# A gated state-space and feed-forward mix on one core: readouts of 12 row blocks moved to ScalarE and adding transfers, two chunks of x turned by VectorE and SyncE transfers

## The chip, the core and the metric

The kernel runs on one core of a Trainium2 chip. A core has TensorE (matmuls, results in PSUM), VectorE (DVE), ScalarE (ACT), GpSimd (POOL) and SyncE (SP). Each takes its instructions in the order in which they stand in its own stream, and waits on semaphores for the others. Transfers are issued by SyncE, ScalarE or GpSimd and are carried out by 16 DMA engines that all of them share. The metric is the device time in microseconds, the median of several runs.

## The reference

x is 2048 tokens of 448 features. Two results are computed from it and mixed row by row with a gate.

```
g = sigmoid(sum(x * gate_w))                       # one number a token
dt = exp(log_dt);  Lam_bar = exp(dt * Lambda)      # 448 complex states
Bu = x @ (((Lam_bar - 1) / Lambda)[:, None] * B).T
h[t] = Lam_bar * h[t-1] + Bu[t]                    # over 2048 tokens
a = 2 * Re(h @ C.T) + x * Dskip
b = silu(x @ w1) @ w2                              # 448 -> 1792 -> 448
out = g * a + (1 - g) * b
```

## The kernel before

**Chunks.** The tokens go in 4 chunks of 512 (`tc`), each of 4 row blocks of 128 (`tb`, 16 in all). x lies in `xnat` with tokens on the partitions. The products need it with features on the partitions: `xT`, 4 groups of 128 features (the fourth overlaps the third by 64).

**Turning x.** Chunk 0 is turned by `x0_transposes`, chunks 1 to 3 by `x_transposes(tc, who)`: 32 small transposes on TensorE into two PSUM banks (line 508), then two copies out of PSUM, by VectorE (516) or ScalarE (518). They stand in the list of products at a place given by hand (`fill`).

**Products.** `x_products` takes a list of tiles two at a time. A tile is 128 columns of w1 (`F(tc)`, 14 tiles a chunk) or 64 states of B as real and imaginary part (`B(tc)`, 7 tiles). A pair of tiles takes 14 matmuls on 64 rows (663) into two banks; the first half of pair k+1 is put ahead of the second half of pair k. `evict` brings F tiles through silu into `aT` on ScalarE, and B tiles into `UG`, on VectorE for chunk 0 and on ScalarE for the others.

**The recurrence.** `lanes(tc)` multiplies by cosines and sines (704), so that a real decay is left, scans along the tokens with it (736, seven scans a chunk), casts the result with GpSimd's transfers from `Gf` into `UG` (390), and turns back with the same sines into `H[tc]`. For chunk 0 the products before the scans are made slot by slot (lines 712 to 725), for the others on whole tiles. `gin` carries the state to the next chunk.

**Parameters.** `parameters` makes decay, sines and cosines from three rows that are loaded into `prm`, turned by four tiny matmuls on TensorE (536).

**The sums.** `gates(tc)` makes the gate and puts g * x * Dskip into `Tb`, which is the same memory as `xnat`. `ffn2(tb)` is the second product of the feed-forward part (774): ScalarE scales it by 1 - g into `fe` (780), and GpSimd's transfer adds `fe` to `Tb` (782). `readout(tb)` is the product of the states with C (795): VectorE makes g * product + `Tb` into `ot` (798), and SyncE stores `ot` (801). The last row block is cut in three.

**Order.** The body at lines 864 to 883 lists the work as TensorE does it. `P.add` notes every instruction with what it reads and writes, a cost and a priority. `Plan.order` plays this through: TensorE keeps the listed order; on the other engines the one that can start first goes next, and among those the lowest priority number. The streams are fixed before the kernel runs. Names (`xT2_0`, `H3_5`) stand for pieces of memory: a reader waits for the last writer, a writer for all readers.

`H[3]` also serves as the landing place of B (`Bnat`) at the start. `ct` holds two pairs of f32 rows for the readout weights (`readout_weights`, 822 and 825, used by 827 and 830).

Of the kernel before, what the change touches and what calls it, by code (L numbers as in the profile page):

```python
# [7 lines left out]
ALU = mybir.AluOpType  # L8
# [268 lines left out]
def bass_gated_mix__ssm_conv_s5__dense_activation_silu__prompt_kernel(nc, A_x, A_Lambda_re, A_Lambda_im, A_B_re, A_B_im, A_C_re, A_C_im,  # L277
               A_log_dt, A_Dskip, B_x, B_w1, B_w2, gate_w, out):
    with ExitStack() as ctx:
# [114 lines left out]
        def load_w1(q, k, a, b):  # L394

            cols = slice(w1cuts[k], w1cuts[k + 1])
            src = B_w1[320:448, cols] if a == 3 else B_w1[128 * a:128 * b, cols].rearrange("(b p) f -> p b f", p=128)
            load(q, w1s[:, 3, cols] if a == 3 else w1s[:, a:b, cols], src, " ".join(f"w1_{k}_{i}" for i in range(a, b)),
                 256 * (b - a) * (cols.stop - cols.start))
# [12 lines left out]
        load("sp", Bnat[:, 0:3, :], A_B_re[0:384, :].rearrange("(b p) d -> p b d", p=128), "H3_0 H3_1 H3_2", 384 * 896)  # L412
# [55 lines left out]
        def x0_transposes(q0, part, who):  # L468

            tk = Ps(2)  # L470

            def mm(pe):
                for q in (q0, q0 + 1):
                    for k in range(2):
                        o = ((q - q0) * 2 + k) * 64
                        for h in range(2):
                            p = slice(64 * h, 64 * h + 64)
                            r = pe.transpose(bk(tk, h).bitcast(BF16)[:, o:o + 64], xnat[p, 2 * part + k, XCOL[q]:XCOL[q] + 128], ident[p, p])  # L478
                return r
# [14 lines left out]

        xn_of = {tc: {q: [f"xT{tc}_{h}" for h in range(2)] for q in range(4)} for tc in range(1, NCH)}
        xn_of[0] = {q: [f"xT0_{q}{part}{h}" for part in range(2) for h in range(2)] for q in range(4)}

        def x_transposes(tc, who):
# [13 lines left out]
            for h in range(2):  # L512
                src = lambda h=h: bk(tk, h).bitcast(BF16).rearrange("p (q b n) -> p q b n", q=4, b=4)
                dst = xT[:, :, tc * CH:(tc + 1) * CH].rearrange("p q (b h n) -> p q b h n", h=2, n=64)[:, :, :, h, :]
                if who[h] == "d":
                    DVE(lambda e, src=src, dst=dst: e.tensor_copy(dst, src()), [tk], [f"xT{tc}_{h}"], 0.69, 2.2, "xTe")
                else:
                    ACT(lambda e, src=src, dst=dst: e.activation(dst, src(), AF.Copy), [tk], [f"xT{tc}_{h}"], act_cost(1024), 2.2, "xTe")

        cosn = [f"COS{k}" for k in range(4)] + ["COSd"]  # L520
# [126 lines left out]
        def x_products(tiles, fill={}, wait=()):  # L647
# [10 lines left out]
            def steps(k, h, a, z):  # L658
                def body(pe):
                    for n, cut in list(enumerate(part[h]))[a:z]:  # L660
                        for b, ((i, p0), tile) in enumerate(zip(cut, pairs[k])):
                            tc = tile[1]
                            r = pe.matmul(bk(toks[k], b), weights(tile, p0, p0 + 64, i), xT[p0:p0 + 64, i, tc * CH:(tc + 1) * CH],  # L663
                                          start=(h == 0 and n == 0), stop=(h == 1 and n == 2))
# [41 lines left out]
        def lanes(tc):  # L706
# [4 lines left out]
            t = f"L{tc}"  # L711
            if tc == 0:
                for b in range(4):
# [12 lines left out]
            else:  # L726
# [59 lines left out]
        def readout(tb):  # L786
# [3 lines left out]
            for n, (a, b) in enumerate(cuts):  # L790
                tk = Ps()

                def mm(pe, tk=tk, a=a, b=b):
                    for s in range(NSLOT):
                        r = pe.matmul(bk(tk)[:, 0:b - a], H[tc][:, s, o:o + 128], CP[:, s, a:b], start=(s == 0), stop=(s == NSLOT - 1))  # L795
                    return r
                PE(mm, [f"H{tc}_{s}" for s in range(7)] + [f"CP{s}" for s in range(NSLOT)], [tk], NSLOT * (0.0025 + (b - a) / 2400), f"C{tc}")
                DVE(lambda e, tk=tk, a=a, b=b: e.scalar_tensor_tensor(ot[tb % NOT][:, a:b], bk(tk)[:, 0:b - a], g[:, tb:tb + 1],  # L798
                                                                      Tb[:, tb, a:b], ALU.mult, ALU.add),
# [61 lines left out]
        def C(*tbs):  # L861
# [17 lines left out]
        x_products(F(2, 1) + B(3) + F(3), {1: xt(3, "aa"), 9: [lambda: gates(3), lambda: lanes(3)]})  # L879
        for f in C(4, 5, 6, 7) + G(8, 9, 10, 11):  # L880
# [38 lines left out]
```

## Time and profile before

| what | us |
|---|---|
| median of 3 runs (141.49 to 141.81) | 141.78 |
| the profiled execution, its own time | 141.25 |
| its span, first to last instruction | 139.5 |
| TensorE, both products with xT (663) | 48.5 + 25.8 |
| TensorE, second feed-forward product (774) | 43.2 |
| VectorE, all scans (736), 28 of them | 33.8 |
| ScalarE, silu out of PSUM (634) | 28.7 |

The granted TensorE clock was 0.998 of full speed. The span is the stretch that the profile tells of; the rest of the time lies around it. Of the products with xT two matmuls on 64 rows run side by side, so a pair of them follows the last pair after 0.216 us though each is shown as 0.376. How full the DMA engines were, and what the queues did:

```profile
DMA  4998999510156770104976200674202322323242
q0 software_dynamic: 6064, 5.51, 24.8%
q1 hardware_dynamic: 11318, 8.65, 20.7%
```

The first line has the mean busy share of the 16 DMA engines in 40 equal slices of the span, in tenths. q0 is GpSimd's queue, q1 SyncE's: packets, megabytes, and their time as a share of all 16 engines' span. The loads fill the engines in the first fifth of the span; later there are mostly GpSimd's casts and adds.

### The profile page before, as it was taken

The numbers are of one execution on the slowest core, as the hardware profiler recorded it, in microseconds if no ns is written. First come the engines' busy times: TensorE is split into PE (matmuls) and PEld (weight loads), VectorE is DVE, ScalarE is ACT, GpSimd is POOL, SyncE is SP. The second block draws the span as 40 slices with busy tenths as digits, with TensorE's granted clock in tenths as the row PEclk, the third lists the DMA queues.
The fourth block names the chain that finished last, engine by engine and source line by source line (L and its number), as shares of the span: only waits on it lengthen the run. The fifth ranks groups of instructions, "written<-read, shape, count | busy, mean of one in ns | idle before, by whom it ended". The sixth has DMA issues, their size and how long they took to land.

```text
span 139.5 us, 3000 instructions
## 1 busy us (share of the span) xinstructions
PE 135.9 (97%) x1201; PEld 67.0 (48%) x1201; DVE 122.0 (87%) x179; ACT 90.3 (65%) x157; POOL 39.2 (28%) x72
## 2 busy tenths in 40 slices
PE   7999999999999999999999999999999999999992
PEld 2445454455544544455544544444455555555561
DVE  0319999999999999999999999999999999997053
ACT  3349768999989999823694887799931268312300
POOL 7134040100248440227733001824000314022220
PEclk9999999999999999999999999999999999999999
DMA  4998999510156770104976200674202322323242
GB/s 136 337 294 243 363 320 238 177 42 0 31 79 94 129 110 1 38 15 73 157 131 155 38 5 0 95 133 79 38 4 97 66 33 36 83 83 61 40 94 71
DMA packets 17956, 14.71 MB, mean 105 GB/s; under 512 B 2835, under 2 KB 17814, under 8 KB 17942
## 3 DMA queue, kind: packets, MB, share of 16 engines
q0 software_dynamic: 6064, 5.51, 24.8%
q1 hardware_dynamic: 11318, 8.65, 20.7%
q10 hardware_dynamic: 560, 0.36, 0.8%
q8 instruction: 9, 0.15, 0.4%
q14 instruction: 5, 0.04, 0.1%
HBM read 7.17 MB, written 1.84 MB: 65 GB/s over the span
## 4 chain that ended last, share of the span: by engine, by line
PE 97%; DVE 0%; issue 0%
PE ps L663 46%; PE ps L774 31%; PE ps L795 15%; PE ps L463 2%; PE ps L508 1%; PE ps L478 1%; PE ps L814 1%; PE ps L604 1%; DVE ot L798 0%; PE ps L675 0%; PE ps L464 0%; PE ps L536 0%
## 5 line engine op out<-in xcount | busy, mean ns | idle before, releaser
L663 PE MATMUL ps<-xT,w1s 64*128 64x512 bf16 x392 | 48.5, 378 | 0.0
L774 PE MATMUL ps<-w2s,aT 128*128 128x448 bf16 x224 | 43.2, 353 | 0.0
L634 ACT ACTIVATE aT<-ps 128x1024 bf16<-128x1024 f32 (+1 forms) x30 | 28.7, 969 | 8.5 <-PE ps L663 8.4
L774 PEld LDWEIGHTS ps<-w2s,aT 128*128 128x128 bf16 x224 | 21.7, 98 | 20.4 <-ACT xnat L849 0.4
L663 PEld LDWEIGHTS ps<-xT,w1s 64*128 64x128 bf16 x392 | 19.7, 94 | 22.3 <-DVE xT L486 0.7
L663 PE MATMUL ps<-xT,BT 64*128 64x512 bf16 x196 | 25.8, 376 | 0.0
L782 POOL DMA_DIRECT2D xnat<-fe x16 | 14.1, 900 | 37.9 <-ACT fe L780 37.2
L780 ACT ACTIVATE fe<-ps,g 128x448 bf16<-128x448 f32 x16 | 10.1, 632 | 21.1 <-PE ps L774 21.0
L390 POOL DMA_DIRECT2D UG<-Gf x27 | 14.7, 549 | 20.9 <-DVE Gf L736 20.4
L736 DVE TENSOR_TENSOR_SCAN Gf<-rc,gin,H 128x512 f32<-128x512 f32 x14 | 17.2, 1268 | 0.0
L795 PE MATMUL ps<-CP,H 128*128 128x448 bf16 (+2 forms) x98 | 16.4, 326 | 0.0
L663 PEld LDWEIGHTS ps<-xT,BT 64*128 64x128 bf16 x196 | 10.8, 94 | 11.1 <-DVE Gf L562 0.2
L798 DVE SCALAR_TENSOR_TENSOR ot<-ps,g,xnat 128x448 bf16<-128x448 f32 (+2 forms) x18 | 10.8, 622 | 6.0 <-issue 4.6
L390 POOL DMA_DIRECT2D UG<-UG x8 | 4.8, 597 | 29.2 <-ACT UG L642 17.4
L704 DVE TENSOR_TENSOR H<-UG,COS 128x3584 bf16<-128x3584 bf16 (+4 forms) x10 | 12.6, 1266 | 0.0
L795 PEld LDWEIGHTS ps<-CP,H 128*128 128x128 bf16 x98 | 8.9, 98 | 7.5 <-DVE k L752 0.4
L642 ACT ACTIVATE UG<-ps 128x1024 bf16<-128x1024 f32 (+1 forms) x12 | 10.7, 923 | 1.4 <-PE ps L663 1.4
L842 ACT ACTIVATE junk<-xg 128x448 bf16<-128x448 bf16 x16 | 9.2, 574 | 2.1 <-DVE xg L704 2.0
L849 ACT ACTIVATE xnat<-xnat,g 128x448 bf16<-128x448 bf16 x16 | 9.8, 671 | 0.2
L704 DVE TENSOR_TENSOR PI<-UG,SIN 128x512 bf16<-128x512 bf16 (+2 forms) x13 | 9.1, 722 | 0.0
L704 DVE TENSOR_TENSOR PO<-UG,SIN 128x1536 bf16<-128x1536 bf16 (+1 forms) x8 | 8.7, 1087 | 0.1
L736 DVE TENSOR_TENSOR_SCAN Gf<-rc,gin,H2C 128x512 f32<-128x512 f32 x7 | 8.5, 1265 | 0.0
(102 smaller groups left out, 126.5 us busy)
## 6 DMA issues: line engine op xcount, KB each, us to landing
UG<-Gf POOLq DMA_DIRECT2D x21, 128.0 KB, 2.5
xnat<-fe POOLq DMA_DIRECT2D x16, 112.0 KB, 2.6
out_dram<-ot SPq DMA_DIRECT2D x15, 112.0 KB, 1.7
w2s<-in_B_w_dram SPq DMA_DIRECT2D x1, 1568.0 KB, 11.8
xnat<-in_A_x_dram SPq DMA_DIRECT2D x3, 448.0 KB, 6.1
w1s<-in_B_w_dram SPq DMA_DIRECT2D x1, 576.0 KB, 6.2
UG<-UG POOLq DMA_DIRECT2D x8, 64.0 KB, 2.2
H2C<-in_A_C_re_dram SPq DMA_DIRECT2D x2, 196.0 KB
```

Of the source, the lines that this page charges most:

```text
L390: P.add(q, lambda e: e.dma_start(dst, src), list(after), name.split(), 0.6 if q == "pool" else 0.5, prio, sem(), nbytes, tag="ld " + name)
L634: ACT(lambda e, src=src, dst=dst: e.activation(dst, src(), AF.Silu), [tk, "tbl"], [f"aT{tc % 2}_{m}" for m in names], act_cost(512 * n), 2 ...
L642: ACT(lambda e, src=src, dst=dst: e.activation(dst, src(), AF.Copy), [tk], [f"{un}{m}" for m in names], act_cost(512 * n), 5, "U")
L663: r = pe.matmul(bk(toks[k], b), weights(tile, p0, p0 + 64, i), xT[p0:p0 + 64, i, tc * CH:(tc + 1) * CH], start=(h == 0 and n == 0), stop=( ...
L704: DVE(lambda e: e.tensor_tensor(o, a, b, op), r, w, dve_cost(n, 2), prio, tag)
L736: DVE(lambda e, s=s, b=b, init=init: e.tensor_tensor_scan(Gf[:, s, :], rc[:, b:b + 1].to_broadcast([128, CH]), A[:, s, :], init, ALU.mult, ...
L774: r = pe.matmul(bk(tk)[:, 0:D_MOD], aT[tc % 2][:, fb, o:o + 128], w2s[:, fb, :], start=(fb == 0), stop=(fb == NFB - 1))
L780: ACT(lambda e: e.activation(f[:, :], bk(tk)[:, 0:D_MOD], AF.Copy, scale=g1[:, tb:tb + 1]), [tk, f"g1_{tc}"], [fn], act_cost(448, 1), 7, "fe")
L782: P.add("pool", lambda e: e.dma_start(Tb[:, tb, :], f[:, :], accum_op=ALU.add), [fn, f"Tb{tb}"], [f"Tb{tb}"], 0.94, 2, sem(), 115000, tag= ...
L795: r = pe.matmul(bk(tk)[:, 0:b - a], H[tc][:, s, o:o + 128], CP[:, s, a:b], start=(s == 0), stop=(s == NSLOT - 1))
L798: DVE(lambda e, tk=tk, a=a, b=b: e.scalar_tensor_tensor(ot[tb % NOT][:, a:b], bk(tk)[:, 0:b - a], g[:, tb:tb + 1], Tb[:, tb, a:b], ALU.mul ...
L849: ACT(lambda e, tb=tb: e.activation(Tb[:, tb, :], xnat[:, tb, :], AF.Copy, scale=g[:, tb:tb + 1]), [f"xd{tc}", f"g_{tc}"], [f"Tb{tb}"], ac ...
```

## The change

- Chunks 2 and 3 are no longer turned by TensorE. `x_blocks(tc)` turns 32x32 blocks on VectorE into a scratch in `H[3]` (4 instructions), and 16 transfers on SyncE's queue bring each block of rows to its place in `xT`, 32 partitions and 64-byte runs at a time. The turning of chunk 2 is ordered behind a product of chunk 0's lanes (`PI_0`), that of chunk 3 behind chunk 0's result (`H0_0`); both use the same scratch.
- The readouts of row blocks 0 to 11 are scaled by g out of PSUM by ScalarE into `ct` (f32). GpSimd's transfer adds them to `Tb`, and SyncE stores `Tb` itself. Blocks 12 to 15 stay as they were.
- Chunk 0's lanes are made on whole tiles as the others are.
- w1's loads are cut otherwise (two halves a column group, the second of which takes feature groups 2 and 3 in one transfer; the second column group partly on ScalarE's queue), the parameter rows are loaded ahead of w1's third column group, and `parameters` stands half a pair earlier in TensorE's list. Chunk 1 is turned one pair earlier, and chunk 0's lanes are listed one pair later.
- `xT` is laid out chunk by chunk.

```diff
+L0M = True
+XT1K = 6
+S0 = (0, 4, 1, 5, 2, 6, 3)
+XT1 = "da"
+XPRIO = {2: 15, 3: 20.5}
+XBLK = (2, 3)
+XBEH = {2: "PI_0", 3: "H0_0"}
+UDVE = (0, 1, 2, 3, 4, 5, 6)
+OUTA = tuple(range(12))
+PRMF = (0, 0)
...
-        xT = sb("xT", [128, 4, S_TOK], BF16)
+        xT = sb("xT", [128, NCH, 4, CH], BF16)
...
-        load_w1("sp", 0, 0, 2)
-        load_w1("act", 0, 2, 3)
-        load_w1("act", 0, 3, 4)
-        for k in range(1, len(w1cuts) - 2):
-            load_w1("sp", k, 0, 3)
-            load_w1("sp", k, 3, 4)
+        for k in range(2):
+            load_w1("sp", k, 0, 2)
+            load_w1("act", k, 2, 4)
         for k, v in enumerate((A_log_dt, A_Lambda_re, A_Lambda_im)):
             load("sp", prm[k:k + 1, 0:448], v.rearrange("(o n) -> o n", o=1), f"prm{k}", 896)
+        load_w1("sp", 2, 0, 2)
+        load_w1("sp", 2, 2, 4)
...
+        def x_blocks(tc):
+            X32 = H[3][:, 0:4, :].rearrange("p m (q b i) -> p m q b i", q=4, i=32)
+            names = [f"X32_{k}" for k in range(4)]
+            held = [f"H3_{s}" for s in range(7)] + ["H3_3i"]
+            turned = [f"BT{s}_{h}" for s in range(7) for h in range(2)]
+            xs = xnat[:, 4 * tc:4 * tc + 4, :]
+            for k, (q0, q1, c, b0, b1) in enumerate(((0, 3, 0, 0, 2), (0, 3, 0, 2, 4), (3, 4, XCOL[3], 0, 2), (3, 4, XCOL[3], 2, 4))):
+                n = q1 - q0
+                src = xs[:, b0:b1, c:c + 128 * n].rearrange("p b (q m i) -> p b q m i", q=n, i=32)
+                dst = X32.rearrange("p m q b i -> p b q m i")[:, b0:b1, q0:q1, :, :]
+                DVE(lambda e, dst=dst, src=src: e.transpose(dst, src), [f"xn{tc}", XBEH[tc]] + turned, [names[k]], 0.15 + 256 * n / 960, XPRIO[tc], "xTd")
+            k = sem()
+            for g in range(4):
+                for m in range(4):
+                    to = xT[32 * m:32 * m + 32, tc, :, :].rearrange("p q (b g i) -> p (q b) g i", b=4, i=32)[:, :, g, :]
+                    P.add("sp", lambda e, to=to, g=g, m=m: e.dma_start(to, X32[32 * g:32 * g + 32, m, :, :, :].rearrange("p q b i -> p (q b) i")),
+                          names + held, [f"xT{tc}_{g}{m}"], 0.66, 400, k, 32768, tag="xTm")
...
-            if tc == 0:
+            if tc == 0 and not L0M:
...
+                if tb in OUTA:
+                    f, fn = ct[tb // 2 % 2][:, tb % 2, :], f"ct{tb // 2 % 2}{'ab'[tb % 2]}"
+                    ACT(lambda e, tk=tk, f=f: e.activation(f, bk(tk)[:, 0:D_MOD], AF.Copy, scale=g[:, tb:tb + 1]),
+                        [tk, f"g_{tc}"], [fn], act_cost(448, 1), 3, "out")
+                    P.add("pool", lambda e, f=f: e.dma_start(Tb[:, tb, :], f, accum_op=ALU.add), [fn, f"Tb{tb}"], [f"Tb{tb}"], 0.94, 2, sem(), 230000, tag="Tb+")
+                    P.add("sp", lambda e: e.dma_start(out2[t0:t0 + 128, :], Tb[:, tb, :]), [f"Tb{tb}"], [], 0.3, 1, outs[tb % NOT], 128 * 896, tag="st")
+                    continue
...
-                   {(1, 0): [parameters], (K - 2, 0): turn_b[:1], K - 2: turn_b[1:2], K - 1: turn_b[2:], 7: xt(1, "da") + [lambda: lanes(0)]}, [K - 2])
+                   {PRMF: [parameters], (K - 2, 0): turn_b[:1], K - 2: turn_b[1:2], K - 1: turn_b[2:], XT1K: xt(1, XT1), 8: [lambda: lanes(0)] + [lambda: x_blocks(2)] * (2 in XBLK)}, [K - 2])
...
+        if 3 in XBLK:
+            x_blocks(3)
-        x_products(F(1) + F(2, 0, 1) + B(2), {2: xt(2, "aa")})
+        x_products(F(1) + F(2, 0, 1) + B(2), {2: xt(2, "aa")} if 2 not in XBLK else {})
...
-        x_products(F(2, 1) + B(3) + F(3), {1: xt(3, "aa"), 9: [lambda: gates(3), lambda: lanes(3)]})
+        x_products(F(2, 1) + B(3) + F(3), {1: xt(3, "aa") if 3 not in XBLK else [], 9: [lambda: gates(3), lambda: lanes(3)]})
```

More of the change, by code (lines that the diff above doesn't have):

```diff
@@ L396, in load_w1 @@
             cols = slice(w1cuts[k], w1cuts[k + 1])
-            src = B_w1[320:448, cols] if a == 3 else B_w1[128 * a:128 * b, cols].rearrange("(b p) f -> p b f", p=128)
-            load(q, w1s[:, 3, cols] if a == 3 else w1s[:, a:b, cols], src, " ".join(f"w1_{k}_{i}" for i in range(a, b)),
-                 256 * (b - a) * (cols.stop - cols.start))
+            n = cols.stop - cols.start
+            if b == 4:
+                src = bass.AP(B_w1.tensor, 128 * a * F_FF + cols.start, [[F_FF, 128], [(320 - 128 * a) * F_FF, 2], [1, n]])
+            else:
+                src = B_w1[128 * a:128 * b, cols].rearrange("(b p) f -> p b f", p=128)
+            load(q, w1s[:, a:b, cols], src, " ".join(f"w1_{k}_{i}" for i in range(a, b)), 256 * (b - a) * n)
         for h, q in enumerate(("sp", "act")):
             load(q, xnat[:, 2 * h:2 * h + 2, :], x2[256 * h:256 * h + 256, :].rearrange("(b p) d -> p b d", p=128), f"xn0{h}", 256 * 896)
-        load_w1("sp", 0, 0, 2)
-        load_w1("act", 0, 2, 3)
-        load_w1("act", 0, 3, 4)
-        for k in range(1, len(w1cuts) - 2):
-            load_w1("sp", k, 0, 3)
-            load_w1("sp", k, 3, 4)
+        for k in range(2):
+            load_w1("sp", k, 0, 2)
+            load_w1("act", k, 2, 4)
         for k, v in enumerate((A_log_dt, A_Lambda_re, A_Lambda_im)):
             load("sp", prm[k:k + 1, 0:448], v.rearrange("(o n) -> o n", o=1), f"prm{k}", 896)
+        load_w1("sp", 2, 0, 2)
+        load_w1("sp", 2, 2, 4)
         Bnat = H[3][:, :, 0:D_MOD]
@@ L416, in bass_gated_mix__ssm_conv_s5__dense_activation_silu__prompt_kernel @@
         btn = {s: [f"BT{s}_{h}" for h in range(2)] for s in range(7)}
-        load_w1("sp", len(w1cuts) - 2, 0, 3)
-        load_w1("sp", len(w1cuts) - 2, 3, 4)
+        load_w1("sp", len(w1cuts) - 2, 0, 2)
+        load_w1("sp", len(w1cuts) - 2, 2, 4)
         for dst, src, name in ((gwb, gate_w, "gwb"), (dkb, A_Dskip, "dkb")):
@@ L482, in x0_transposes @@
                 src = lambda h=h: bk(tk, h).bitcast(BF16)[:, 0:256].rearrange("p (q b n) -> p q b n", q=2, n=64)
-                dst = xT[:, q0:q0 + 2, 256 * part:256 * part + 256].rearrange("p q (b h n) -> p q b h n", h=2, n=64)[:, :, :, h, :]
+                dst = xT[:, 0, q0:q0 + 2, 256 * part:256 * part + 256].rearrange("p q (b h n) -> p q b h n", h=2, n=64)[:, :, :, h, :]
                 names = [f"xT0_{q}{part}{h}" for q in (q0, q0 + 1)]
@@ L495, in bass_gated_mix__ssm_conv_s5__dense_activation_silu__prompt_kernel @@
         xn_of = {tc: {q: [f"xT{tc}_{h}" for h in range(2)] for q in range(4)} for tc in range(1, NCH)}
+        for tc in XBLK:
+            xn_of[tc] = {q: [f"xT{tc}_{g}{m}" for g in range(4) for m in range(4)] for q in range(4)}
         xn_of[0] = {q: [f"xT0_{q}{part}{h}" for part in range(2) for h in range(2)] for q in range(4)}
@@ L513, in x_transposes @@
                 src = lambda h=h: bk(tk, h).bitcast(BF16).rearrange("p (q b n) -> p q b n", q=4, b=4)
-                dst = xT[:, :, tc * CH:(tc + 1) * CH].rearrange("p q (b h n) -> p q b h n", h=2, n=64)[:, :, :, h, :]
+                dst = xT[:, tc, :, :].rearrange("p q (b h n) -> p q b h n", h=2, n=64)[:, :, :, h, :]
                 if who[h] == "d":
@@ L638, in evict @@
                 dst = U[:, sl, :]
-                if tc == 0:
+                if tc == 0 and a in UDVE:
                     DVE(lambda e, src=src, dst=dst: e.tensor_copy(dst, src()), [tk], [f"{un}{m}" for m in names], 0.15 + 0.53 * n, 2.6, "U")
@@ L662, in body @@
                             tc = tile[1]
-                            r = pe.matmul(bk(toks[k], b), weights(tile, p0, p0 + 64, i), xT[p0:p0 + 64, i, tc * CH:(tc + 1) * CH],
+                            r = pe.matmul(bk(toks[k], b), weights(tile, p0, p0 + 64, i), xT[p0:p0 + 64, tc, i, :],
                                           start=(h == 0 and n == 0), stop=(h == 1 and n == 2))
@@ L711, in lanes @@
             t = f"L{tc}"
-            if tc == 0:
+            if tc == 0 and not L0M:
                 for b in range(4):
@@ L732, in lanes @@
                 tt(A[:, :, :], A[:, :, :], PI[:, :, :], ALU.add, pin, als, 3584, pr, t)
-            for s in (3, 0, 4, 1, 5, 2, 6) if tc else (0, 4, 1, 5, 2, 6, 3):
+            for s in (3, 0, 4, 1, 5, 2, 6) if tc else S0:
                 b = s if s < 4 else s - 4
```

## The prediction, before the result was known

> **What bounds the kernel now.** I read the page's busy times first, then the chain that ended last in order of time, then the queues and the timeline of each engine around the places that the change touches.
>
> ```profile
> PE 135.9 (97%) x1201; PEld 67.0 (48%) x1201; DVE 122.0 (87%) x179; ACT 90.3 (65%) x157; POOL 39.2 (28%) x72
> PE 97%; DVE 0%; issue 0%
> ```
>
> TensorE is busy for 97% of the span, and the chain that ended last is TensorE from start to end. So what TensorE no longer does comes off the time, and what any other engine gains or loses counts only where TensorE has to wait for it. The chain in order of time:
>
> ```profile
> 40.15 5.40 PE ps L663 x50
> 45.55 0.47 PE ps L508 x32
> 46.02 11.22 PE ps L663 x104
> 57.24 10.70 PE ps L774 x56
> 67.94 5.30 PE ps L795 x28
> 73.24 3.99 PE ps L663 x36
> 77.23 0.47 PE ps L508 x32
> 131.38 5.35 PE ps L795 x42
> ```
>
> Columns are start, length, work. There is no gap from piece to piece. L508 is the turning of one chunk of 512 tokens of x; the second and third of the three such pieces are chunks 2 and 3. The product matmuls run at 11.22/104 = 0.108 us each.
>
> **Part 1, TensorE.** The turning of chunks 2 and 3 leaves it: 2 x 0.47 = 0.94 us off the path. Nothing is added to it.
>
> **Part 2, the replacement for chunk 2, and when it is due.** VectorE turns 32x32 blocks (4 instructions a chunk: two of 768 elements a row, two of 256), then SyncE issues 16 transfers of 32 KB a chunk, each 512 pieces of 64 bytes. The due time: the list F(1), one tile of F(2), B(2) starts at 40.15; seven pairs of 14 matmuls are chunk 1, but the first half of the eighth pair runs ahead of the last 6 of them, so chunk 2 is first read after 92 matmuls, 40.15 + 92 x 0.108 = 50.1. VectorE's timeline gives the earliest start:
>
> ```profile
> 27.51 0.68 DVE L704 TENSOR_TENSOR H<-UG,COS 128x1024 bf16<-128x1024 bf16 x1
> 30.39 0.68 DVE L827 SCALAR_TENSOR_TENSOR CP<-ps,sc1s,ct 128x448 bf16<-128x448 bf16 x1
> 35.20 1.21 DVE L736 TENSOR_TENSOR_SCAN Gf<-rc,H 128x512 f32<-128x512 f32 x1
> 55.82 2.02 DVE L704 TENSOR_TENSOR H<-H,PO 128x3584 bf16<-128x3584 bf16 x1
> ```
>
> Chunk 0's lanes start at 27.51. Made whole as in the other chunks, they are 2.01 + 0.95 + 1.22 us (rows of L704 at 3584, 1536 and 2048 elements) up to the product that the turning is ordered behind: 31.7. The first two readout weights at 30.39 still go ahead (1.2): 32.9. No row shows a VectorE transpose: its bounds are the copy of 1024 bf16 elements at 0.68 and the cast of 1024 f32 at 1.22, that is 0.7 to 1.2 ns an element, and 0.29 for a copy of 256. A chunk is then 2 x 0.55 + 2 x 0.29 = 1.7 up to 2 x 0.95 + 2 x 0.4 = 2.7; I take 2.6, by the f32 tensor_tensor row (512 elements in 0.68), since it is one element a step. The blocks are ready at 35.5, or at 34 if the parameters (part 5) pull VectorE forward by the 1.6 us that they come earlier. I go on with 34.8.
>
> Issues on SyncE: the loads of short rows took 0.54 to 0.87, median 0.64 (H2C from C_im); plain ones 0.43. 16 x 0.64 = 10.2, bounds 6.9 and 13.9. SyncE's queue is empty from 22.95 to 70.30, so nothing stands in front. Landing 1.7 (a store) to 2.8 (UG from UG). So chunk 2 lands at 34.8 + 10.2 + 1.7 = 46.7, or up to 51.5 with both upper bounds. That leaves 3.4 us, and minus 1.4 at worst: from there each us late is a us of the whole kernel.
>
> What a 64-byte piece costs an engine is not shown. The nearest are 128-byte rows from HBM. A quarter of a microsecond in which they were most of the traffic, and a second with rows of 896 bytes almost alone:
>
> ```profile
> DMA packets 162, 0.08 MB, mean 303 GB/s; under 512 B 104, under 2 KB 157, under 8 KB 162
> q1 hardware_dynamic: 154, 0.06, 84.9%
> q1 hardware_dynamic: 435, 0.38, 108.9%
> ```
>
> The second: 1.089 x 16 / 435 = 40 ns a row of 896 bytes. The first: 0.849 x 16 x 0.25 = 3.4 us for 154, of which 50 large ones take 2.0, so 13.5 ns for a short one. 32 pieces and a semaphore on each of 16 engines: 33 x 13.5 = 0.45 us a transfer, below the 0.64 of its issue, so the issue sets the pace. The upper bound is 41 ns, no cheaper than a large row: 1.35 us, 21.6 for the chunk. I take the lower, as it was measured with short rows, and keep the other as a rival.
>
> **Part 3, chunk 3.** Its turning stands behind the last write of chunk 0's result, at 55.82 + 2.02 = 57.8, moved by 2.6 (part 2) less 1.7 (part 4), less up to 1.6 from the start: 57 to 59. Then 2.6 + 10.2 + 2.8: landed by 74.6. It is due after 78 matmuls of the list that starts at 73.24 - 0.47: 81.2. It is hidden with 6 us to spare. It also waits until chunk 2's transfers have read the shared buffer (47 to 50); behind it on VectorE are chunk 1's lanes, which TensorE reads at 99.50 only and which are done at 86.2.
>
> **Part 4, what VectorE and ScalarE swap.**
>
> ```profile
> L798 DVE SCALAR_TENSOR_TENSOR ot<-ps,g,xnat 128x448 bf16<-128x448 f32 x15 | 9.9, 673 | 5.9 <-issue 4.6 <-PE ps L795 1.3
> L780 ACT ACTIVATE fe<-ps,g 128x448 bf16<-128x448 f32 x16 | 10.1, 632 | 21.1 <-PE ps L774 21.0
> L782 POOL DMA_DIRECT2D xnat<-fe x16 | 14.1, 900 | 37.9 <-ACT fe L780 37.2 <-ACT xnat L849 0.7
> L518 ACT ACTIVATE xT<-ps 128x1024 bf16<-128x1024 bf16 x5 | 4.9, 1028 | 0.0
> ```
>
> VectorE loses 12 x 0.673 = 8.1, loses 1.7 by whole products in chunk 0 (2.0 + 0.4 + 2.7 + 2.7 against 2.0 + 0.95 + 1.2 + 2.0), gains 2 x 2.6: net -4.6. ScalarE gains 12 x 0.632 = 7.6 and loses 4 x 1.03: net +3.5 on 90.3. GpSimd gains 12 issues of 0.9 (the source has twice the bytes; I add nothing for that, as the issue is what is busy). All of it beside TensorE. Cover: the last readouts start at 131.38 and their input is done at 128.2, 3.2 us early, and VectorE gets 4.6 more; without that cover a late end would cost one for one. ScalarE is full from 67.5 to 73.7 around blocks 0 to 3, and 2.5 more pushes the next due eviction (75.76, after 2.08 idle) back by 0.5, against eight PSUM banks: nothing. Each new add waits for the earlier add of its rows, long landed for blocks 0 to 7; for 8 to 11 by 121. Behind these adds on GpSimd stand the casts of chunk 1's scans; GpSimd idles 5.1 us from 68 to 76 against 3.6 added, and chunk 1 has 13 us. The stores wait for the adds; the last, block 11, is out by 127 against an end at 138.
>
> **Part 5, the start.** The three parameter rows go past one w1 load on SyncE, and one load less is ahead of them: issued 1.6 us earlier, they land near 6.5 for a turn on TensorE now due at 7.1. The 512-column w1 load goes back by 0.35 (landed 7.6, first read 7.8, now 8.1). Value 0, bounds -0.1 (the wait for the second w1 part) and +0.4.
>
> **Sum.** 139.5 - 0.94 = 138.6 of span, and the 1.75 around it: 140.3 for the profiled execution, whose 141.25 lay 0.5 under the median of 141.78. Against that median: 140.8.
>
> **Rivals.** (A) The gain is eaten: chunk 2 lands 0.5 to 1.4 late by the bounds of part 2, or the start loses 0.4: about 141.8. For it: the 3.4 us hang on a start that I placed by hand. Against it: both bounds must meet.
>
> (B) The slower one: GpSimd's queue and the small pieces share the 16 engines. From 35 to 52 us that queue alone shows
>
> ```profile
> q0 software_dynamic: 1739, 1.50, 58.0%
> UG<-UG POOLq DMA_DIRECT2D x2, 64.0 KB, 6.4
> ```
>
> 0.58 x 17 x 16 / 1739 = 91 ns a packet, 109 packets an engine: 9.9 us. If an engine does one at a time, with the small pieces' 528 x 13.5 = 7.1 on top, chunk 2 lands at 34.8 + 17 + 1.7 = 53.5: 3.4 late, 141.78 - 0.94 + 3.4 = 144.2. It decides once the two together pass 13.6 us. For it: the second line (around 18 to 20 us) shows 64 KB taking 6.4 us among loads where 2.2 is usual. Against it: issues spread the pieces, a third of GpSimd's work falls after 46, and shares above 100% show that packets overlap. The Trainium skill, DMA: Bandwidth & Descriptors, section on queues, rings and completion order, has each engine take turns between its queues packet by packet; by that rule a 64-byte piece may stand behind a 91 ns packet each time, which is this rival.
>
> (C) Small pieces cost 41 ns: 34.8 + 21.6 + 1.7 = 58.1, 8 late, 148.8; it decides from 26 ns. For it, only the mean of mixed stretches. The same page's Specifications ask for 512 bytes and put a read-modify-write below that, which speaks for it; its section on small descriptors excepts transfers within SBUF, which speaks against. No row of this case has such pieces within SBUF.
>
> (D) The turning does not do what it is placed for: ScalarE's readouts hold banks and TensorE waits some 0.5, about 141.4. Against it: the bank count above.
>
> **Chances.** Forecast 0.62 (own range 140.3 to 141.3), A 0.13, D 0.04, B 0.15, C 0.06. A measurement here tells from no change what is beyond 0.3%, 0.43 us. So faster 0.62, within 0.17 (A and D), slower 0.21 (B and C). The range goes up through A and D into the low part of B: 140.2 to 143.4.
>
> **What would show it.** Right: two pieces of L508 gone from the chain, no wait of a product matmul on a transfer near 50 and 81 us, busy TensorE about 0.9 lower. Wrong: an idle of the weight loads released by the xT transfers (B, C, told apart by what the small packets took and by how GpSimd's landings lengthen), or VectorE's turning after 36 us (A).

## The result, and the profile after

The changed kernel took 146.36 us (median of 6 runs, 145.11 to 147.75) against 141.87 for the kernel before in the same sitting (6 runs, 141.49 to 142.43): a ratio of 1.027, 95% interval 1.021 to 1.034. (Ratios here and below leave out executions more than 1.5% above the fastest of their kernel, here those at 147.62 and 147.75; medians hold all of them.) The forecast was 140.8, and its range ended at 143.4. The profiled execution took 147.62 with a span of 145.8, so 6.3 us of span came on top of 139.5. The medians lie 4.5 us apart; the sum below is that of the profiled execution. In the two runs at 145.11 and 145.62 the granted clock stayed at full speed; in the other four its mean was 0.984 to 0.988.

The page of the changed kernel has the busy times and, as tenths of full speed, the granted TensorE clock in 40 slices of the span:

```profile
PE 137.3 (94%) x1137; PEld 67.9 (47%) x1137; DVE 118.9 (82%) x161; ACT 92.7 (64%) x165; POOL 49.2 (34%) x84
PEclk9999999999999999999999999995999999999999
```

TensorE runs 64 matmuls less, yet is busy for 1.4 us more, and idle for 8.5 us of the span where it was for 3.6. One slice has the clock at half. The small pieces are there: the trace has 16,384 packets of 64 bytes on SyncE's queue. What TensorE's matmuls waited for, in us in total, times, and the longest:

```profile
PE ps L697 <- ACT aT L668: 3.0, 1, 3.0
PE ps L697 <- DMA xT<-H: 1.2, 1, 1.2
PE ps L697 <- DMA w1s<-in_B_w_dram: 0.5, 1, 0.5
```

All three are new: at 95 us a wait for an eviction by ScalarE (an eviction is the copy that frees a PSUM bank), at 82 us one for chunk 3's transfers, near 8 us one for w1's third column group. The table counts on the starts of the matmuls, with what each distance is over the usual one, which gives 0.1 to 0.2 us more than the rows of the view. Waits in the experiments are counted the same way where no row is shown.

| where | us of span |
|---|---|
| the two turnings of L508 are gone | -0.94 |
| start: the second group of readout weights is turned at 34.60, before at 33.85 (early among the runs, as the section on the start shows) | +0.75 |
| chunk 3's first product starts late | +1.3 |
| wait for banks before 98.5 | +3.2 |
| then 8 pairs of products at 0.421 us a pair, 0.216 before | +1.6 |
| from the last matmul to the end, 3.15, before 2.75 | +0.4 |
| sum | +6.3 |

How the long wait came about is in the timelines (start, length, work, in brackets the idle time before and what ended it). VectorE first, the kernel before and then the changed one:

```profile
89.64 1.06 DVE L704 TENSOR_TENSOR xg<-xnat,gwb 128x1792 bf16<-128x1792 bf16 x1
```

```profile
82.83 0.96 DVE L738 TENSOR_TENSOR PO<-UG,SIN 128x1536 bf16<-128x1536 bf16 x1 [3.10 <-DMA UG<-Gf]
85.24 1.23 DVE L738 TENSOR_TENSOR PO<-UG,SIN 128x2048 bf16<-128x2048 bf16 x1 [1.45 <-DMA UG<-Gf]
95.73 1.07 DVE L738 TENSOR_TENSOR xg<-xnat,gwb 128x1792 bf16<-128x1792 bf16 x1
```

Then ScalarE, and TensorE behind it (the cut is marked):

```profile
96.83 0.58 ACT L883 ACTIVATE junk<-xg 128x448 bf16<-128x448 bf16 x1 [4.83 <-DVE xg L738]
97.41 1.00 ACT L668 ACTIVATE aT<-ps 128x1024 bf16<-128x1024 f32 x1
...
98.47 5.70 PE L697 MATMUL ps<-xT,w1s 64*128 64x512 bf16 x36 [3.00 <-ACT aT L668]
```

VectorE stood 4.55 us while it turned chunk 1's scans back, waiting for GpSimd's casts of them. So it came to chunk 3's gate product (xg) at 95.73; before it was at 89.64. ScalarE's in-order list has the first of the sums over that product (L883; these sums are called the z sums below) ahead of the next eviction (L668). It stood 4.83 us; the full banks were freed after it, and TensorE stood 3.0.

Why the casts were late: the stretch from 70 to 80 us, before and then after (busy time of PE, PEld, DVE, ACT, POOL; the last three numbers are clock, DMA share, GB/s):

```profile
70.00:80.00 10.00, 10.00 (x110) 4.87 (x109) 9.91 (x17) 7.27 (x13) 2.02 (x4) 1.00 0.55 110
```

```profile
70.00:80.00 10.00, 10.00 (x81) 4.61 (x81) 9.64 (x15) 8.80 (x22) 7.60 (x11) 1.00 1.16 137
```

The DMA queues and issues of the same stretch (queue rows: packets, MB, share of 16 engines; issue rows: count, KB each, median us from issue to landing), before:

```profile
q0 software_dynamic: 720, 0.64, 39.7%
UG<-Gf POOLq DMA_DIRECT2D x3, 128.0 KB, 2.5
```

After:

```profile
q0 software_dynamic: 1326, 1.13, 87.5%
q1 hardware_dynamic: 3504, 0.22, 27.7%
UG<-Gf POOLq DMA_DIRECT2D x6, 128.0 KB, 6.1
xT<-H SPq DMA_DIRECT2D x6, 32.0 KB, 6.2
```

And the mean share of the 16 engines in 40 slices of this stretch, after:

```profile
DMA  9999759989999999899999999999999999999999
```

The engines' share goes from 0.55 to 1.16 (above 1 means that packets of one engine overlap in time), and 36 of the 40 slices are at 90% or more, where 15 were before: they have hardly a break. A cast takes 6.1 us where it took 2.5. Chunk 3's transfers are issued from 62.89 on, first some 0.65 apart; from 70.3 on four of the last five issues take 1.1 to 1.7 each. The last one lands at 83.17.

### The profile page after: what moved, and what is told of

Read it like the earlier page. It is cut to its first block, busy times and chain, and to the rows that moved or that the text cites. A ratio compares the mean times of both kernels' runs of the same rounds, so it can differ in the third digit from the quotient of the medians.

```text
span 145.8 us, 2919 instructions
## 1 busy us (share of the span) xinstructions
PE 137.3 (94%) x1137; PEld 67.9 (47%) x1137; DVE 118.9 (82%) x161; ACT 92.7 (64%) x165; POOL 49.2 (34%) x84
## 4 chain that ended last, share of the span: by engine, by line
PE 29%; DVE 13%; POOL 6%; DMA 5%; issue 3%; ACT 1%; DVEq 0%; POOLq 0%
PE ps L808 15%; PE ps L829 10%; DMA UG<-Gf 5%; PE ps L697 5%; DVE Gf L770 3%; POOL UG L400 3%; DVE H L738 3%; DVE H2C L738 3%; POOL xnat L836 2%; DVE H L546 1%; DVE ot L839 1%; DVE PO L738 1%; DVE PI L738 1%; DVE xg L738 1%; POOL xnat L816 1%
## 5 line engine op out<-in xcount | busy, mean ns | idle before, releaser
L697 PE MATMUL ps<-xT,w1s 64*128 64x512 bf16 x392 | 50.4, 390 | 4.6 <-ACT aT L668 3.0
L697 PEld LDWEIGHTS ps<-xT,w1s 64*128 64x128 bf16 x392 | 20.7, 97 | 28.6 <-issue 3.6
L668 ACT ACTIVATE aT<-ps 128x1024 bf16<-128x1024 f32 (+1 forms) x30 | 28.6, 960 | 8.3 <-PE ps L697 8.3
L808 PEld LDWEIGHTS ps<-w2s,aT 128*128 128x128 bf16 x224 | 21.7, 98 | 20.4 <-issue 0.4
L814 ACT ACTIVATE fe<-ps,g 128x448 bf16<-128x448 f32 x16 | 10.2, 634 | 21.0 <-PE ps L808 19.0
L400 POOL DMA_DIRECT2D UG<-Gf x27 | 15.4, 574 | 14.8 <-DVE Gf L770 14.3
L697 PEld LDWEIGHTS ps<-xT,BT 64*128 64x128 bf16 x196 | 11.4, 94 | 10.6 <-DVE Gf L596 0.2
L836 POOL DMA_DIRECT2D xnat<-ct x12 | 11.0, 961 | 7.8 <-ACT ct L834 7.3
L883 ACT ACTIVATE junk<-xg 128x448 bf16<-128x448 bf16 x16 | 9.2, 576 | 5.9 <-DVE xg L738 5.9
L738 DVE TENSOR_TENSOR H<-UG,COS 128x3584 bf16<-128x3584 bf16 (+2 forms) x7 | 12.1, 1745 | 0.0
L839 DVE SCALAR_TENSOR_TENSOR ot<-ps,g,xnat 128x448 bf16<-128x448 f32 (+2 forms) x6 | 3.0, 526 | 10.6 <-PE ps L829 10.5
L890 ACT ACTIVATE xnat<-xnat,g 128x448 bf16<-128x448 bf16 x16 | 10.4, 666 | 0.3
L834 ACT ACTIVATE ct<-ps,g 128x448 f32<-128x448 f32 x12 | 7.6, 631 | 2.5 <-PE ps L829 2.5
```

The lines of the kernel that those rows point to most:

```text
L400: P.add(q, lambda e: e.dma_start(dst, src), list(after), name.split(), 0.6 if q == "pool" else 0.5, prio, sem(), nbytes, tag="ld " + name)
L738: DVE(lambda e: e.tensor_tensor(o, a, b, op), r, w, dve_cost(n, 2), prio, tag)
L808: r = pe.matmul(bk(tk)[:, 0:D_MOD], aT[tc % 2][:, fb, o:o + 128], w2s[:, fb, :], start=(fb == 0), stop=(fb == NFB - 1))
L814: ACT(lambda e: e.activation(f[:, :], bk(tk)[:, 0:D_MOD], AF.Copy, scale=g1[:, tb:tb + 1]), [tk, f"g1_{tc}"], [fn], act_cost(448, 1), 7, "fe")
L836: P.add("pool", lambda e, f=f: e.dma_start(Tb[:, tb, :], f, accum_op=ALU.add), [fn, f"Tb{tb}"], [f"Tb{tb}"], 0.94, 2, sem(), 230000, tag=" ...
L890: ACT(lambda e, tb=tb: e.activation(Tb[:, tb, :], xnat[:, tb, :], AF.Copy, scale=g[:, tb:tb + 1]), [f"xd{tc}", f"g_{tc}"], [f"Tb{tb}"], ac ...
```

## The experiments

The theory after reading the trace (S in the expectations): the casts of chunk 1's scans land late among chunk 3's pieces and the new adds, VectorE falls behind by them and by its turning, chunk 3's gate product comes late, ScalarE's z sums stand ahead of evictions, TensorE runs out of banks, and its clock falls. Against it stood that the new adds alone do it (P), that VectorE's turning and order alone do it (V), and that evictions of B(3), not the z sums, hold the banks (E). All runs are compared with the kernel before on the same chip in the same sitting (its medians there: 141.67, 141.74, 141.71, 141.71). Line numbers shift by one or two where an edit adds or takes lines.

**Which part makes the loss.** Four kernels take one part each out of the changed one. `pe3`: chunk 3 is turned by TensorE again.

```diff
-XBLK = (2, 3)
+XBLK = (2,)
```

> Chunk 3 is turned by TensorE again, all else as changed. Theory S (the 16 DMA engines are over-full from 70 to 80 us, share 1.16, by chunk 3's 64-byte pieces, the new adds and chunk 1's casts together; the casts land up to 7.6 us after issue instead of 2.5, and through VectorE, the evictions and ScalarE's order TensorE waits 3.2 at 95 us and runs slow for 1.6 after it): casts land within 4 us, no wait near 81 or 95, 141.87 - 0.47 + 0.64 (start) = 142.0, 141.5 to 142.8. Rival P (the four new adds on GpSimd's queue alone do it): the wait at 95 stays, about 145.5. Rival V (VectorE reaches chunk 1 3.7 us later, by its turning and order): the turning of chunk 3 is gone here too, so 142 to 143.5, which does not tell it from S.

Measured: 141.71 (141.28 to 142.17), ratio 1.000 [0.998, 1.003]. No wait at 82 or 95; 1.0 us at the start. The range of S is met, and P is out, for the adds are all there. The large loss is gone with chunk 3 back on TensorE, while chunk 2 is still turned by VectorE.

`outa0`: all readouts by VectorE, as before, both chunks turned by VectorE.

```diff
-OUTA = tuple(range(12))
+OUTA = ()
```

> All readouts leave by VectorE again, no new adds; both chunks still turned by VectorE and transfers. Theory S: the adds are about a third of the load from 70 to 78 us, so casts land in 3 to 5 us, the wait on chunk 3 shrinks below 1.0, the one at 95 to below 2: 142 to 144.5. Rival P: both waits go, 141.87 - 0.94 + 0.64 = 141.6. Rival V: VectorE gets 2.7 us more to do from 69 to 78, so the wait at 95 stays or grows: 146 to 148.

Measured: 142.23, ratio 1.005 [1.003, 1.007]. No wait at 82 or 95 either. Instead the readout of chunk 3 waits 1.1 us at 130.5 for chunk 3's result, since VectorE has its 8 us of readouts back. Without the adds chunk 3 lands at 79.42, so its wait at 82 hangs on them. The missing wait at 95 says less: xg is at 93.21, but ScalarE's list has two more evictions ahead of the z sums here.

`turn_only`: VectorE turns chunk 3, but no transfer takes it away; TensorE turns it too, and its result is used.

```diff
-        for tc in XBLK:
+        for tc in (2,):
...
-            for g in range(4):
+            for g in range(4 if tc == 2 else 0):
...
-        ... {1: xt(3, "aa") if 3 not in XBLK else [], 9: ...
+        ... {1: xt(3, "aa"), 9: ...
```

> VectorE turns the blocks of chunk 3 as in the changed kernel, but its 16 transfers are left out and TensorE turns chunk 3 for use. Theory S: as with chunk 3 on TensorE, 141.5 to 142.8, no wait at 95. Rival P: 145.5. Rival V: VectorE's load is that of the changed kernel, so the wait at 95 stays: 145 to 146.5.

Measured: 143.08, ratio 1.008 [1.005, 1.011], a wait of 1.45 near 94 us and VectorE waiting 2.5 for the casts. Neither theory has its range: S had no wait, V 145 and more. The turning costs 1.4 us over `pe3`, together with what the planner moves around it in the lists of VectorE, ScalarE and GpSimd. The rest of the loss comes with the transfers: in the traces of `turn_only` and of the change the lists of VectorE and GpSimd are the same.

`move_only`: the 16 transfers are issued behind the same result, but copy the scratch as it is to chunk 0's place in xT, which nobody reads any more; VectorE leaves chunk 3's turning out, and TensorE does it. The lists of VectorE, ScalarE and GpSimd are those of `pe3`.

```diff
-                DVE(lambda e, dst=dst, src=src: e.transpose(dst, src), ...
+                if tc == 2: DVE(lambda e, dst=dst, src=src: e.transpose(dst, src), ...
-                    to = xT[32 * m:32 * m + 32, tc, :, :]...
+                    to = xT[32 * m:32 * m + 32, tc if tc == 2 else 0, :, :]...
...
-                          names + held, ...
+                          names + held + ["H0_0", "CP3"] * (tc == 3), ...
```

> The 16 transfers of chunk 3 are issued at the same place but move what lies in the scratch to a place that nobody reads; VectorE does not turn chunk 3, TensorE does. Theory S: engines over-full as before, casts land 6 us and more after issue, the wait at 95 stays, only the one at 81 is gone: 144.5 to 146.5. Rival P: the same. Rival V: VectorE is 2.4 us earlier: 142 to 143.

Measured: 142.06, ratio 1.003 [1.000, 1.006], 0.2 us of wait at 92. That is V's range, and S's is missed: with all the small pieces and all the adds there, little is lost when VectorE does not spend 2.5 us on the turning. But this is not the load of the change. With no turning ahead of them the transfers are issued 3.8 us earlier (from 59.12 on, against 62.89), the last lands at 75.81, and the longest cast takes 5.5 us instead of 7.6. What casts as late as in the change do to a VectorE that turns nothing is not shown. The parts side by side, from the traces:

| kernel | adds of blocks 0 to 3 | small pieces of chunk 3 | VectorE turns chunk 3 | longest cast, 60 to 82 us | VectorE waits for casts, 74 to 96 us | xg of chunk 3 | TensorE's waits near 82 / 95 |
|---|---|---|---|---|---|---|---|
| before | no | no | no | 3.3 | 0 | 89.64 | 0 / 0 |
| outa0 | no | yes | yes | 3.7 | 0 | 93.21 | 0 / 0 |
| pe3 | yes | no | no | 5.4 | 0 | 89.25 | 0 / 0 |
| turn_only | yes | no | yes | 5.7 | 2.5 | 93.26 | 0.3 / 1.45 |
| move_only | yes | yes, 3.8 us earlier | no | 5.5 | 1.5 | 90.11 | 0 / 0.2 |
| after | yes | yes | yes | 7.6 | 4.6 | 95.73 | 1.3 / 3.2 |

The adds lengthen the casts by 2 us, the pieces alone by 0.4, both at the same time most. The turning, with what the planner moves around it, puts xg later by some 4 us. With all three xg is latest, and only there does TensorE wait 3.2 us. How much of the 6 us of lateness belongs to the turning and how much to the casts is not divided further by these runs.

**Is it ScalarE's order?** `z_late`: as the change, but chunk 3's z sums stand behind the last evictions. In the traces only ScalarE's list differs: those of the other engines are the same, instruction for instruction.

```diff
-                    ["xg"], ["junk", f"zl{tc}"], ...
+                    ["xg"] + ["aT1_13"] * (tc == 3), ["junk", f"zl{tc}"], ...
-        ... 9: [lambda: gates(3), lambda: lanes(3)]})
+        ... 16: [lambda: gates(3), lambda: lanes(3)]})
```

> As the changed kernel, but ScalarE's four row sums of chunk 3's gate stand behind all evictions of chunk 3's F tiles instead of among them; nothing else moves. Theory T (the wait at 95 is VectorE's lateness at chunk 3's gate product, started at 89.2 with chunk 3 on TensorE, 90.1, 93.3 and 95.7 in the four other profiles with waits of 0, 0.2, 1.4 and 3.2 us, handed on by ScalarE's fixed order): no wait at 95 and no slow clock after it, the one for chunk 3 near 81 stays: 142.3 to 143.3. Rival E (the late evictions of chunk 3's B tiles hold the banks, whatever ScalarE does next): the wait stays, 145 or more.

Measured: 142.85, ratio 1.008 [1.005, 1.011], where the change has 1.027: 2.7 us come back, by the ratios. xg is as late as ever (95.02), but ScalarE evicts ahead of it, the wait at 95 is gone and the clock is whole. The wait for chunk 3's transfers stays. One of ScalarE's evictions, and the wait of TensorE:

```profile
91.81 1.02 ACT L668 ACTIVATE aT<-ps 128x1024 bf16<-128x1024 f32 x1 [0.49 <-PE ps L697]
PE ps L697 <- DMA xT<-H: 1.1, 1, 1.1
```

So the long wait and the half clock come from ScalarE's z sums standing ahead of evictions while xg is late. The evictions of B(3) keep their order here, and they hold nothing up.

**Chunk 3 earlier.** `turn_early`: chunk 3 is turned right behind chunk 2, into the dead chunk 0 of xT, and sent off between 46 and 58 us.

```diff
-XPRIO = {2: 15, 3: 20.5}
+XPRIO = {2: 15, 3: 15.5}
-XBEH = {2: "PI_0", 3: "H0_0"}
+XBEH = {2: "PI_0", 3: "PI_0"}
...
-            X32 = H[3][:, 0:4, :]...
+            X32 = (H[3][:, 0:4, :] if tc == 2 else xT[:, 0, :, :])...
...
+        if 3 in XBLK:
+            x_blocks(3)
         gates(0)
...
```

> Chunk 3 is turned right behind chunk 2 into a scratch of its own (the dead part of xT that held chunk 0), so its transfers go out from 45 to 56 us, ahead of chunk 1's casts and the new adds. Theory T: no wait near 81; casts of chunk 1 land 3 to 5.5 us after issue, as without chunk 3's transfers; VectorE is at chunk 3's gate product near 93, wait at 95 of 0 to 1.5 without a slow clock: 141.6 to 143.0. If the place of the transfers does not matter: 145 to 147.

Measured: 143.95, ratio 1.017 [1.012, 1.022]. The wait at 82 is gone, but chunk 0's work on VectorE moves back, and a wait of 1.5 us for a late eviction appears at 56.6, with 1.4 left at 95. So the waits near 81 and 95 came out as expected, and the time did not: a new wait came with the turning's earlier place.

**The start.** `old_start` puts back the loads of w1 and of the parameters, and the parameters' place in TensorE's list; the rest is the change. `pe3_old_start` does the same to `pe3`.

```diff
-PRMF = (0, 0)
+PRMF = (1, 0)
...
-        for k in range(2):
-            load_w1("sp", k, 0, 2)
-            load_w1("act", k, 2, 4)
+        load_w1("sp", 0, 0, 2)
+        load_w1("act", 0, 2, 3)
+        load_w1("act", 0, 3, 4)
+        for k in range(1, len(w1cuts) - 2):
+            load_w1("sp", k, 0, 3)
+            load_w1("sp", k, 3, 4)
...
-        load_w1("sp", 2, 0, 2)
-        load_w1("sp", 2, 2, 4)
...
```

> w1 and parameter loads and the place of the parameters as before the change, all else as changed. The start's part is the wait of 0.64 at 8.0 us (w1's third column group behind the parameter rows): it goes, the waits at 81 and 95 stay: 145.7, 145.0 to 147.0. If the loads are not its cause: 146.4.

> Chunk 3 turned by TensorE and the loads as before the change; chunk 2 by VectorE and transfers, readouts of 12 blocks by ScalarE. All causes found so far are out, one turning of 0.47 is saved: 141.7 (chunk 3 on TensorE) less 0.65 (its waits below 9 us, 1.1, against 0.5 before) = 141.0, 140.7 to 141.4. If the loads are not the cause of the start's wait: 141.7.

Measured: 149.11, ratio 1.052 [1.048, 1.056], and 149.14, ratio 1.050 [1.046, 1.055]. Neither came near its figure. In `old_start` TensorE now stands where it had not, 3.8 us at its longest, for chunk 2's transfers near 50 us:

```profile
PE ps L695 <- DMA xT<-H: 4.4, 2, 3.8
```

Its timeline of VectorE has the reason:

```profile
33.12 2.02 DVE L736 TENSOR_TENSOR H<-UG,COS 128x3584 bf16<-128x3584 bf16 x1
35.05 1.83 DVE L544 STREAM_TRANSPOSE H<-xnat 128x768 bf16<-128x768 bf16 x2
36.80 0.64 DVE L866 SCALAR_TENSOR_TENSOR CP<-ps,sc1s,ct 128x448 bf16<-128x448 bf16 x1
39.14 0.76 DVE L544 STREAM_TRANSPOSE H<-xnat 128x256 bf16<-128x256 bf16 x2
```

With the parameters later the planner puts a product of chunk 1 ahead of chunk 2's turning and readout weights in the middle of it. It ends at 39.9, in the change at 34.3, and SyncE's 16 issues begin only then.

Three kernels ask what the start itself costs. `pe3_w1` is `pe3` with w1's third group ahead of the parameters, its second half on ScalarE's queue; `pe3_w1_vec` has all readouts by VectorE besides; `read_only` leaves both chunks to TensorE and keeps the readouts, the whole products and the start.

```diff
+        load_w1("sp", 2, 0, 2)
+        load_w1("act", 2, 2, 4)
         for k, v in enumerate((A_log_dt, A_Lambda_re, A_Lambda_im)):
...
-        load_w1("sp", 2, 0, 2)
-        load_w1("sp", 2, 2, 4)
```

> As pe3 (chunk 2 turned by VectorE, chunk 3 by TensorE, twelve readouts by ScalarE), but w1's third column group (columns 512 to 1023) is loaded ahead of the three parameter rows, its second half by ScalarE's queue; the order of the work on TensorE and VectorE is that of pe3. If the 1.0 us that TensorE waits near 8 us in pe3 is that load coming behind the parameters, the wait falls to 0.2 or less and the time to 140.8 to 141.2, below before. If the wait is the HBM loads as such, whatever their order, it stays at 0.6 or more and the time at 141.7.

> As pe3_w1, but all readouts leave by VectorE as before, so that of the change only chunk 2's turning by VectorE and what serves it is left. If ScalarE's readouts and their adds do good or nothing by themselves: 140.9 to 141.4. If VectorE, which has 8.1 us more, comes late at the end (as with outa0, 1.1 us at 130.5): 141.8 to 142.3.

> The twelve readouts by ScalarE, their adds, chunk 0's whole products and the moved loads, but x's chunks 2 and 3 turned by TensorE. If the adds do harm only together with VectorE's turning and the small transfers: no wait at 81 and 95, the start's 0.6 to 1.0 alone, 142.3 to 142.8. If the adds and the late casts alone make VectorE late: a wait over 1 us near 95, 143.3 or more.

Measured: 142.36, ratio 1.004 [1.001, 1.007]; 142.70, ratio 1.003 [0.999, 1.006]; 142.49, ratio 1.004 [1.001, 1.007]. In `pe3_w1` the wait only moves: 0.66 us for the parameters instead of 1.0 for w1. The wait stayed as its second arm had it, for another load, and the time was above both arms: this swap does not mend the start. `pe3_w1_vec` is not told from no change; its profiled execution had w1's second group 2.9 us late, so that trace says nothing of the readouts. `read_only` met the first arm: ScalarE's readouts and their adds alone make no wait at 82 or 95. In its profile the start costs 0.5, and the end is 0.7 longer than before.

`mend`: the change with blocks 0 to 3 read out by VectorE, the z sums as in `z_late`, the loads as in `pe3_w1`, and semaphores of their own for the stores of ScalarE's blocks. `loads_old` is `mend` with the loads of before but the parameters' new place in TensorE's list.

```diff
-OUTA = tuple(range(12))
+OUTA = tuple(range(4, 12))
```

> Both chunks turned by VectorE as in the change, with three mends: blocks 0 to 3 are read out by VectorE as before (their four adds come off GpSimd's queue from 68 to 76 us, blocks 4 to 11 stay with ScalarE), ScalarE's z sums of chunk 3 stand behind the evictions (as in z_late), w1's third group is loaded ahead of the parameters. If the wait at 81 comes from the transfers meeting adds and casts, the one at 95 from ScalarE's order, and the one at 8 from the order of the loads, all three go: 140.8 to 141.4, below before. If chunk 3's small pieces and chunk 1's casts are enough for the wait at 81 without the adds: 1 us more, 141.8 to 142.4.

> As mend, but the loads of w1 and of the parameters are those of before, in their old order, while TensorE still turns the parameters after 16 product matmuls. VectorE's order stays that of the change. If the loads set the start: the parameters land near 8 us (8.16 before), TensorE waits 1.0 to 1.4 us for them near 7, no wait at 50: 142.0 to 142.6. If the old loads by themselves made chunk 2 late in old_start: a wait of 1 us or more near 50, 143 or more.

Measured: `mend` 141.69, ratio 1.000 [0.998, 1.002]; `loads_old` 141.22, ratio 0.998 [0.995, 1.000]. Both times the waits at 82 and 95 are gone: the last transfer of chunk 3 lands at 79.84 and 80.36, the longest cast takes 4.3 and 3.8. `mend` missed its figure: against before, its profile has 0.7 more at the start and 0.5 more at the end. `loads_old` came out below the 142.0 that its first arm began with: its wait for the parameters is 0.75 us and not 1.0 to 1.4. What TensorE waits for in it, apart from 0.8 at the very start as in any kernel here, and 0.2 for a load of w1:

```profile
PE ps L568 <- DVE prm L570: 0.6, 1, 0.6
```

Its second group of readout weights is turned at 34.70, 0.85 later than before. From there to the end of the span it is 104.7 against 105.6: 0.9 less, nearly the whole of the 0.94. By its medians (141.22 against 141.71) 0.49 of it is left, and the interval of the ratio just reaches no change. It is the best version of the study.

Last, `turn_first` is `mend` with loads and parameters' place of before, but chunk 2's turning put early by hand; `pe3_turn_first` does this to `pe3`.

```diff
-XPRIO = {2: 15, 3: 20.5}
+XPRIO = {2: 0.5, 3: 20.5}
-XBEH = {2: "PI_0", 3: "H0_0"}
+XBEH = {2: "PI_4", 3: "H0_0"}
```

> As mend, but the loads and the parameters' place on TensorE are those of before, and VectorE turns chunk 2 right behind chunk 0's second product, ahead of the third and of the other readout weights. If old_start lost its 5 us to VectorE's order alone, there is no wait near 50; the start costs what it costs before, 0.5 us of waits up to 10 us instead of 1.1 to 1.3: 140.9 to 141.3. If the old start itself is what makes chunk 2 late: 2 us or more of wait at 50, 143.5 or more.

> As pe3 (chunk 2 by VectorE, chunk 3 by TensorE, twelve readouts by ScalarE), with loads, parameters' place and chunk 2's early turning as in turn_first. By the order theory: before less 0.47 of TensorE and the old start: 141.1 to 141.4. If the old start makes chunk 2 late: 143.5 or more.

Measured: 143.20, ratio 1.010 [1.007, 1.013], and 145.02, ratio 1.015 [1.010, 1.020]. Chunk 2 lands at 48.53 and 48.03 and there is no wait at 50, so it was the order and not the loads. Neither reached its figure. `pe3_turn_first` turns its second group of readout weights at 33.87, as the kernel before, but `turn_first` only at 35.08, after 1.6 us of waiting for a late load of w1: the start scatters. And both kernels have a new wait at 43 us, 1.6 and 2.3 long. ScalarE in `turn_first`:

```profile
41.48 0.63 ACT L862 ACTIVATE ct<-ps,scc 128x448 f32<-128x448 bf16 x1 [0.89 <-DVE CP L870]
44.48 0.63 ACT L812 ACTIVATE fe<-ps,g 128x448 bf16<-128x448 f32 x1 [1.49 <-DMA xnat<-fe]
```

The readout weights on VectorE now stand behind the turning and two products. ScalarE waits for their buffers, its feed-forward readouts come behind that and wait for their own adds, and TensorE's banks with them. In `turn_first` chunk 3's transfers come 0.4 late as well (landed at 84.33). With the parameters at their old place chunk 0's lanes begin at 28.74 in `turn_first` and at 27.54 in `pe3_turn_first`; with the old loads but the new place, in `loads_old`, at 26.81. VectorE is then too late for the weights or for the turning.

## Why the prediction was wrong, step by step

**Part 1** was right: 0.94 less, as the trace of `loads_old` shows after its start. The sum failed on what stands beside it.

**Part 2** was right in what it concluded. The four turning instructions took 2.48 us (2.6 taken), a single issue 0.64 at the median (0.64), a 64-byte piece 11 ns at the median (13.5). Three issues took 0.8 to 1.2 and the last landing 2.6 instead of 1.7, so chunk 2 landed at 48.35 instead of 46.7. The slack covered that: chunk 2 was due at 50.1 by the forecast and was first read at 50.7, with no wait. Rival C is thereby out.

**Part 3** failed in one term: "landed by 74.6", and with it "hidden with 6 us to spare". Issue and landing were carried over from a quiet stretch, and the load that was already there was not read. From 62.9, the first issue, to 81.2, when chunk 3 was due by the forecast, the DMA engines' share was 0.59 before, that is 10.8 of 18.3 us. On it come 8192 pieces of 11 ns (5.6 us of all 16 engines) and four adds of 128 packets at 126 ns (4.0), medians of the trace after: an estimate of 20.4 us of work in 18.3. Part 4's "I add nothing for that" is in this too: such a packet took 93 ns from a bf16 source. The share after is 1.00 in that stretch. Chunk 3 landed at 83.17, 8.6 later than reckoned: 1.3 by a later first issue, 2.5 by slower issues (12.7 for 10.2), 4.7 by the last landing (7.5 for 2.8).

**Part 4** failed in its cover, and this is the larger error. "GpSimd idles 5.1 us from 68 to 76 against 3.6 added" weighed GpSimd's issuing and not the transfers that it issues. "Chunk 1 has 13 us", and part 3's "which TensorE reads at 99.50 only", followed chunk 1's result to TensorE alone. VectorE itself waits for the casts, and what is next on VectorE, chunk 3's gate product, is read by ScalarE at a point of its in-order list that stands ahead of evictions. `z_late` shows that this path, not the lanes, made the long wait. That it takes the casts and the turning together to be late enough fits `pe3`, `turn_only` and `move_only`, but no run has the casts of the change without the turning. The push of ScalarE against eight banks, valued at "nothing", was the right place to look, but rival D gave it half a microsecond from ScalarE's own load.

**Part 5** was put at 0, at most +0.4. Its price is not settled to better than some tenths. The second group of readout weights was turned at 34.01 to 34.70 in eleven profiled kernels with the parameters' new place (median 34.39), and in the five with the old one at 33.85 to 35.08 (median 34.01): 0.4, with a scatter as large. By the medians of the times `loads_old` keeps 0.5 of its 0.94, which again leaves 0.4. `read_only`, which gains nothing on TensorE, is 0.8 over before, but that holds its longer end too. So about +0.4, the upper bound. (One profile is left out of this, that of `pe3_w1_vec` with its late load.) What the part missed altogether is what the moved parameters are for: with the old loads and place chunk 2's turning ends 5.6 us later, and its slack of some 2 us is gone.

**The rivals.** B had the mechanism, GpSimd's queue and the small pieces sharing the 16 engines, and the wrong place: it was tried at chunk 2, where it did not happen, and priced at 144.2. At chunk 3 it did. There both queues slowed, the cast from 2.5 to 6.1 us and the small transfer from 2.6 to 6.2. The Trainium skill, DMA: Bandwidth & Descriptors, section on queues, rings and completion order, has each engine take turns between its queues. The trace agrees as far as it goes: it shows that both queues slowed, not the turns. Of A the part on the start came true.

**The test that was named** worked: a wait of the products on a transfer near 81, and GpSimd's landings lengthened, were given as the mark of B.

## What to carry to other kernels

Weigh a DMA issue by the engine time of its packets in the stretch where it lands, not by the time its engine takes to issue it; two queues that each fit (87.5% and 27.7% here) can fill the 16 engines together. When work is pushed back, follow it through every in-order list that reads it, and look at what stands behind the reader: here a sum of 0.58 us ahead of an eviction turned a harmless delay into 3.2 us of TensorE and a half clock. A load order that looks like tidying can be what a planner's order rests on: take it back alone before calling it free.

## What the hardware showed that was not expected

**The clock.** A wait of 3.2 us brought the granted clock down for one stretch after it, in the changed kernel (the numbers at the end are clock, DMA share, GB/s):

```profile
98.50:102.00 3.50, 3.50 (x18) 1.27 (x20) 3.50 (x4) 3.50 (x9) 1.21 (x3) 0.53 0.37 62
```

So did one of 2.3 us, in `pe3_turn_first`:

```profile
44.80:48.50 3.70, 3.70 (x20) 1.33 (x18) 3.70 (x5) 1.73 (x2) 2.49 (x4) 0.54 0.84 114
```

Each cost 1.6 us more than the wait. Longer waits, of 3.9 us in `old_start` and 5.0 in `pe3_old_start`, did it too. Waits of 1.1, 1.45, 1.55 and 1.6 us in `outa0`, `turn_only`, `turn_early` and `turn_first` did not do it. The Trainium skill, TensorE: Matmul & The Clock Gate, section on the clock gate, puts the fall to half speed behind at least one idle window of about 3.4 us; the half speed agrees (pairs at 0.421 us against 0.216), but here one wait of 2.3 us was enough. In the changed kernel it fell in some executions and not in others.

**The end.** From the end of VectorE's last readout to the end of the span it took 2.36 us before, 2.5 to 3.0 in `pe3`, `pe3_w1`, `mend`, `outa0`, `read_only`, `move_only`, `turn_early`, `pe3_turn_first` and the change, and 2.3 to 2.4 in the other kernels. A transfer that brings instructions falls into the last microseconds of many of the first kind, but also into those of `pe3_old_start` and `turn_first`, which end in 2.38. So the cause stays open.
